# Retention and two feed-forward layers on one core: layer one's weights shared by two blocks in groups of 4, 6 and 6 steps in place of 6, 5 and 5

## The chip, the core and the metric

The kernel runs on one core of one Trainium2 chip. The metric is the device time of one execution in microseconds (us). The engines of the core are TensorE (PE, its weight loads shown as PEld), VectorE (DVE), ScalarE (ACT), GpSimd (POOL) and SyncE (SP), whose queue issues nearly all of the DMAs here. Times are medians of several runs; the profile shows one execution by itself.

## The reference, cut to what matters

```
def _attn_ref(q, k, v):                      # (4, 8, 576, 64), float32
    scores = np.matmul(q, k.transpose(0, 1, 3, 2)) / np.sqrt(64)
    gamma = 1.0 - 2.0 ** (-5.0 - np.arange(H))
    rel = pos[:, None] - pos[None, :]
    Dmat = np.where(rel >= 0, gamma[:, None, None] ** rel, 0.0)
    return np.matmul(scores * Dmat, v)

x = attn_out.transpose(0, 2, 1, 3).reshape(2304, 512)
h = x @ w_in1;  g = np.where(h > 0, h, np.exp(np.minimum(h, 0)) - 1);  y = g @ w_out1
h2 = np.maximum(y @ w_in2, 0);  out = (h2 * h2) @ w_out2
```

Both layers have 512 inputs and 2048 hidden units. The weights w_in1, w_out1, w_in2 and w_out2 come as float64 and have to be turned into float32 on the chip.

## The kernel before, in words

The 2304 tokens are cut into five blocks of 512, 512, 256, 512 and 512 tokens (BLOCKS). Every product of layer one is made of three float32r matmuls (mm3, L163 to L165): high part by high part, high by low, low by high. The 2048 hidden units of layer one are 16 pieces of 128, numbered f = 0 to 15.

**A weight unit** is one piece of w_in1 or of w_out1: 128 rows of 512 float64 values, 512 KB. Its way is: a DMA on SP's queue into a raw place (load_raw, L187 or L192); conversion to float32 (to_f32: on ACT L204 and L205, on DVE L206, L207, L208 and a custom instruction at L211); the split into high and low part (split_w: on ACT L159, on DVE L160), after which it stays in SBUF as part of a tile of three units, w0 to w10. There are 32 units, in the order in0, in1, out0, in2, out1, in3, out2, and so on to out15.

**A step** of layer one is a block and a piece f. up(blk, f) makes 12 matmuls into a PSUM tile h (two buffers), then on ACT L365 to L367 and on DVE L369 and L370 the activation, then the split of the result g (L159, L160). down(blk, f) makes 12 matmuls of g with the piece of w_out1 into four PSUM banks; it comes LAG = 2 steps later.

**Groups.** The first two blocks share each weight while it is fresh: the list GROUPS cuts the 16 pieces, and for each group block 0 runs through its pieces and then block 1 through the same pieces (ORDER1). At the end of a group down moves the four banks to SBUF (ACT copies at L404, or DVE adds at L402 where an earlier group's sums are to be added) and to the DRAM tensor parts and back (L394, L406).

**The attention** of a block runs in chunks of up to 128 tokens, each of three pieces: transposes (PE L293, ACT copies L298), scores (PE L306, DVE mask L309) and values (PE L321, L325 and L335; ACT L159 and DVE L160 write the block's x; DVE L341 or L343 update the running state st). Block 0 is done first (the list of twelve pieces with EARLY, which tells how many units are to be split after each of them). Block 1 has five chunks of 64, 128, 128, 128 and 64 tokens, so 15 pieces, and they are spread over the steps that SPREAD[1] names; they must be done before block 1's first step. The two chunks of block 2 follow at the end of the shared steps.

**The pace of conversion.** In the middle of step i (mid, called in up between the activation's ACT and DVE parts) the attention pieces of that step are emitted first and then w1_to(units1(i)): splits are emitted until units1(i) units are done. w1_run, which does it, also emits the loads and the conversions that lie ahead: a unit's conversion is one unit ahead of the splits; the loads are AHEAD_NURSED = 5 units ahead of the conversions while a unit still has a nursery place, and AHEAD = 2 ahead after that, in three rotating buffers raw_p. The nursery (NURSERY) is the SBUF of weight tiles that are not written yet: the raw units 0 to 10 land in the places of w4, w5, w6 and w10. The places of w9, w8 and w7 first hold the second, third and fourth chunk of block 0's attention.

**Order.** Loads of layer one's units and of the chunks' q, k and v stay in the order in which the code emits them on SP's queue. The other instructions are put in order by a scheduler that works before the kernel runs; on the chip each engine takes its instructions in that fixed order.

```
def w1_run(n):
    while at["split"] < min(int(n), len(w1)):
        while at["raw"] < min(at["f32"] + (AHEAD_NURSED if at["raw"] < NURSED else AHEAD), len(w1)):
            step("raw", 99, w1, lambda u: load_raw(*u))
        step("split", at["f32"], w1, split_w)
        step("f32", at["raw"], w1, to_f32)
```

Of the kernel before, what the change touches and what calls it, by code (L numbers as in the profile page):

```python
# [21 lines left out]
NF = DFF // P  # L22
# [6 lines left out]
AHEAD = 2  # L29


NURSERY = (("w4", 3), ("w5", 3), ("w6", 3), ("w10", 2))
NURSED = sum(n for _, n in NURSERY)
AHEAD_NURSED = 5

GROUPS = ((0, 6), (6, 11), (11, 16))
ORDER1 = [(b, f) for lo, hi in GROUPS for b in range(2) for f in range(lo, hi)]
SHARED = len(ORDER1)
ORDER1 += [(b, f) for b in range(2, NB) for f in range(NF)]

SPREAD = {1: (0, 5), 2: (SHARED - 5, SHARED - 1), 3: (SHARED, SHARED + NF - 2), 4: (SHARED + NF, SHARED + 2 * NF - 2)}

EARLY = (0, 0, 0, 1, 1, 2, 3, 4, 5, 6, 6, 7)


def units1(i):
    return 7 + 1.4 * min(i + 1, 5) + 0.85 * max(i - 4, 0)


def units2(i):  # L50
# [76 lines left out]
def tile_kernel(ctx: ExitStack, tc, q, k, v, w_in1, w_out1, w_in2, w_out2, cst, out):  # L127
# [43 lines left out]
    def raw_place():  # L171
# [5 lines left out]
        if len(nursery) == n:  # L177
            tag, k = NURSERY[sum(n >= sum(m for _, m in NURSERY[:i + 1]) for i in range(len(NURSERY)))]
            t = wp.tile([P, k, DM, 2], I32, tag=tag, name="raw")
# [194 lines left out]
    def down(blk, f):  # L374
        n = BLOCKS[blk][1]
        g, w = g_t.pop((blk, f)), w_t[0, 1, f]
        shared = blk < 2
        first, last = (any(f == r[e] - (e == 1) for r in (GROUPS if shared else ((0, NF),))) for e in range(2))
        if first:
            acc_t[blk] = [ps_acc.tile([P, TB], F32, tag="acc", name=f"acc{m}") for m in range(KC)]  # L380

        back = shared and last and f >= GROUPS[0][1]
        end = last and f == NF - 1
# [332 lines left out]
    def load_next(late=False):  # L716
        if at["load"] < len(chunks) and (late or chunks[at["load"]][1] < 2 or chunks[at["load"] - 1][1] >= 2):
            load_chunk(chunks[at["load"]][0])
            at["load"] += 1

    def scale_next():
        if at["scale"] < at["load"]:
            scale_chunk(chunks[at["scale"]][0])
            at["scale"] += 1
# [49 lines left out]
    pieces = ((0, 0), (1, 0), (0, 1), (1, 1), (0, 2), (2, 0), (1, 2), (3, 0), (2, 1), (3, 1), (2, 2), (3, 2))  # L774
    for (c, piece), n in zip(pieces, EARLY):
        first[c][piece]()
# [20 lines left out]
    for i, (blk, f) in enumerate(ORDER1):  # L797
        def mid():
            if i == SPREAD[2][0] - 4:
                load_next(True)  # L800
                load_next(True)
                scale_next()
            for of, (lo, hi) in SPREAD.items():
                if lo <= i < hi:
                    need = 3 * len(blocks[of])
                    for _ in range((i - lo + 1) * need // (hi - lo) - (i - lo) * need // (hi - lo)):
                        attn_step()
            if at["split"] < len(w1):
                w1_to(units1(i))
            elif i >= SHARED and at["f322"] < min(len(w2), units2(i)):  # L810

                step("park", at["f322"], w2, park_w)
                with tc.issue_after(mark[0]):
                    step("f322", at["raw2"], w2, to_f32)
                while at["raw2"] < min(len(w2), at["f322"] + 2):
                    step("raw2", 99, w2, lambda u: load_raw(*u))
            if at["f322"] == len(w2):
                step("park", 99, w2, park_w)
            j = i - (len(ORDER1) - NF)

            with tc.issue_after(mark[0]):
                if j == 6:
                    run(factors(0))
                if 7 <= j < NF and j not in (10, 14):
                    next_inputs()
# [81 lines left out]
```

## Time and profile before

| | |
|---|---|
| median of 3 runs | 896.09 us (892.68 to 896.62) |
| the profiled execution's own time | 890.18 us |
| its span, first to last instruction | 888.0 us |
| mean granted TensorE clock | 0.994 |
| busy: PE, DVE, ACT | 857.4, 686.1, 489.7 us |

The profiled execution is an execution of its own: 2.2 us of its time lie outside its span, and it is 5.9 us below the median of the other runs. Busy times of PE are modelled, because matmuls are pipelined: a row's duration is longer than the distance to the next start, and it is the distance that counts. A timeline row reads: start, duration, engine, line, operation, output and inputs, and in brackets how long the engine had been idle and on what it waited last. DVE rows too overlap by a little (0.69 us each, 0.60 us from start to start).

### The profile page before, as it was taken

How to read it: one execution, taken by the hardware profiler on the slowest of the kernel's cores; microseconds unless marked ns; L12 is line 12 of the kernel's file. 1: busy time of each engine (PE TensorE's matmuls, PEld its weight loads, DVE VectorE, ACT ScalarE, POOL GpSimd, SP SyncE). 2: the span in 40 equal slices, each digit the busy share in tenths (PEclk: the TensorE clock that was granted, in tenths of full speed). 3: DMA queues.
4: the chain of work that ended last, by engine and by line, in shares of the span. 5: the costliest groups of instructions: out<-in, count | busy, mean ns of one | idle time of the engine just before them, and what ended most of it. 6: DMA issues, size and time to landing. Idle time of an engine off the chain costs nothing.

```text
span 888.0 us, 14959 instructions
## 1 busy us (share of the span) xinstructions
PE 857.4 (97%) x5630; PEld 770.8 (87%) x5630; DVE 686.1 (77%) x1391; ACT 489.7 (55%) x961; POOL 9.2 (1%) x12
## 2 busy tenths in 40 slices
PE   8798999999998999999999999999999999999998
PEld 5676788888888988888888898999989989999997
DVE  4898888885667867766779857789874769898984
ACT  3665778673464666655767744556553434444441
POOL 3000000000000000000000000000000000000000
PEclk9999999999999999999999999999999999999999
DMA  9923426383529656534463034499997993444330
GB/s 217 272 54 108 143 96 189 119 213 96 142 61 239 160 156 186 172 109 141 132 226 94 24 111 158 154 328 345 350 323 260 401 345 131 155 147 150 120 131 37
DMA packets 157608, 155.33 MB, mean 175 GB/s; under 512 B 62816, under 2 KB 121312, under 8 KB 157536
## 3 DMA queue, kind: packets, MB, share of 16 engines
q1 hardware_dynamic: 150208, 139.69, 51.8%
q10 hardware_dynamic: 7328, 14.68, 4.6%
q8 instruction: 44, 0.72, 0.4%
q14 instruction: 28, 0.23, 0.1%
HBM read 98.77 MB, written 55.57 MB: 174 GB/s over the span
## 4 chain that ended last, share of the span: by engine, by line
PE 82%; DVE 7%; DMA 5%; ACT 2%; issue 1%; SPq 1%; ACTq 1%; POOL 0%; DVEq 0%
PE m L675 18%; PE A L492 10%; PE acc L163 7%; PE acc L164 7%; PE acc L165 7%; PE h L163 7%; PE h L165 6%; PE h L164 6%; PE D L492 5%; PE B L492 2%; PE ps_o L325 2%; PE ps_o L321 1%; DMA raw<-in_moe_w_in_dram 1%; PE ps_s L306 1%; DMA g<-g2s 1%
## 5 line engine op out<-in xcount | busy, mean ns | idle before, releaser
L675 PE MATMUL m<-wo,S 128*128 128x256 f32 x1512 | 184.2, 285 | 3.4 <-ACT S L159 2.4
L675 PEld LDWEIGHTS m<-wo,S 128*128 128x128 f32 x1512 | 183.3, 193 | 4.2 <-ACT S L159 2.8
L159 ACT CAST S<-g 128x512 fp32r<-128x512 f32 (+1 forms) x144 | 74.6, 565 | 95.7 <-DVE g L659 46.8
L163 PE MATMUL h<-x,w 128*128 128x512 f32 (+1 forms) x320 | 119.8, 376 | 3.6 <-DVE t L370 2.7
L164 PE MATMUL acc<-g,w 128*128 128x512 f32 (+1 forms) x320 | 118.8, 372 | 0.0
L164 PE MATMUL h<-x,w 128*128 128x512 f32 (+1 forms) x320 | 118.5, 370 | 0.2 <-DVE x L160 0.2
L165 PE MATMUL h<-x,w 128*128 128x512 f32 (+1 forms) x320 | 118.6, 371 | 0.0
L165 PE MATMUL acc<-g,w 128*128 128x512 f32 (+1 forms) x320 | 117.5, 370 | 0.0
L492 PE MATMUL A<-T,pair 128*128 128x384 f32 x576 | 112.9, 335 | 2.2 <-DVE go L519 1.3
L163 PE MATMUL acc<-g,w 128*128 128x512 f32 (+1 forms) x320 | 111.5, 376 | 2.8 <-ACT w L159 1.6
L492 PEld LDWEIGHTS A<-T,pair 128*128 128x128 f32 x576 | 100.6, 188 | 4.1 <-DVE go L519 2.1
L160 DVE TENSOR_TENSOR S<-g,S 128x512 fp32r<-128x512 f32 (+1 forms) x144 | 85.9, 621 | 22.3 <-ACT S L159 20.9
L365 ACT ACTIVATE t<-h 128x512 f32<-128x512 f32 (+1 forms) x80 | 44.3, 554 | 79.4 <-PE h L165 72.4
L369 DVE SCALAR_TENSOR_TENSOR t<-e,t 128x512 f32<-128x512 f32 (+1 forms) x80 | 50.8, 635 | 44.9 <-ACT t L367 44.4
L163 PEld LDWEIGHTS h<-x,w 128*128 128x128 f32 x320 | 60.5, 190 | 15.4 <-DVE t L370 3.0
L159 ACT CAST g<-t 128x512 fp32r<-128x512 f32 (+1 forms) x80 | 46.1, 578 | 46.4 <-DVE t L370 45.8
L163 PEld LDWEIGHTS acc<-g,w 128*128 128x128 f32 x320 | 59.4, 188 | 13.8 <-ACT w L159 1.8
L164 PEld LDWEIGHTS h<-x,w 128*128 128x128 f32 x320 | 60.7, 190 | 10.6 <-DVE x L160 0.4
L165 PEld LDWEIGHTS h<-x,w 128*128 128x128 f32 x320 | 60.6, 189 | 10.5 <-DVE w L160 0.2
L164 PEld LDWEIGHTS acc<-g,w 128*128 128x128 f32 x320 | 60.3, 188 | 10.3
L165 PEld LDWEIGHTS acc<-g,w 128*128 128x128 f32 x320 | 60.2, 188 | 10.0
L492 PE MATMUL D<-T,pair 128*128 128x384 f32 x288 | 58.5, 336 | 1.9 <-ACT pair L159 0.6
(88 smaller groups left out, 1280.6 us busy)
## 6 DMA issues: line engine op xcount, KB each, us to landing
g2s<-go SPq DMA_DIRECT2D x48, 384.0 KB, 4.3
g<-g2s SPq DMA_DIRECT2D x36, 512.0 KB, 3.9
raw<-in_moe_w_in_dram SPq DMA_DIRECT2D x32, 512.0 KB, 5.4
raw<-in_moe_w_out_dram SPq DMA_DIRECT2D x32, 512.0 KB, 4.1
wo2s<-wo SPq DMA_DIRECT2D x56, 256.0 KB, 4.0
wo<-wo2s ACTq DMA_DIRECT2D x9, 1536.0 KB, 15.6
w2s<-f SPq DMA_DIRECT2D x32, 256.0 KB, 2.3
f<-w2s SPq DMA_DIRECT2D x32, 256.0 KB, 4.2
```

The source lines that it names most:

```text
L159: nc.scalar.copy(pair_hi, src)
L160: eng.tensor_tensor(out=pair_lo, in0=src, in1=pair_hi.bitcast(F32), op=ALU.subtract)
L163: nc.tensor.matmul(ps, l_hi, r_hi, start=first, stop=False)
L164: nc.tensor.matmul(ps, l_hi, r_lo, start=False, stop=False)
L165: nc.tensor.matmul(ps, l_lo, r_hi, start=False, stop=last)
L306: nc.tensor.matmul(ps[e][:n, p, :n], kT[r, p, :n], qT[r, p, :n], start=True, stop=True)
L321: i = nc.tensor.matmul(ps[:, p, :n], st[:, p, :], qT[:, p, :n], start=p == 0, stop=True, skip_group_check=True)
L325: nc.tensor.matmul(ps[e * D:(e + 1) * D, p, :n], vn[:n, 2 * p + e, :], live[e][:n, p, :n], start=not s, stop=True, skip_group_check=True,)
L365: nc.scalar.activation(t, h, AF.Relu, scale=-1.0)
L369: nc.vector.scalar_tensor_tensor(out=t, in0=e, scalar=1.0, in1=t, op0=ALU.add, op1=ALU.mult)
L492: ins = nc.tensor.matmul(ps, w[:, l, o:o + P], t[:, r, j], start=first and i + j == 0, stop=i + j == 3, skip_group_check=True)
L675: ins = nc.tensor.matmul(m(u, k), l[:, x], w[:, y], start=first and k in (1, 6, 4, 5), stop=j == HF - 1 and i == 2, skip_group_check=True,)
```

## The change

The groups become 4, 6 and 6 pieces long. Block 1's attention is therefore spread over the four steps 0 to 3 and not over 0 to 4, and block 1's first step is step 4 and not step 6. EARLY asks for 6 units before step 0 and not 7. units1 asks for 0.9 unit in each of the steps 0 to 3 and 1.1 unit in each later one; before, it was 1.4 in each of the steps 0 to 4 and 0.85 later. In whole units: split before step 0, 6 (before: 7); after step 3's mid, 9 (12); after step 4's, 10 (14); after step 10's, 17 (19); all 32 after step 24's (26's). The nursery grows from 11 to 20 places by w9, w8 and w7, so that the units 11 to 19 are also loaded up to five ahead and no longer pass through raw_p.

```
-NURSERY = (("w4", 3), ("w5", 3), ("w6", 3), ("w10", 2))
+NURSERY = (("w4", 3), ("w5", 3), ("w6", 3), ("w10", 2), ("w9", 3), ("w8", 3), ("w7", 3))
 NURSED = sum(n for _, n in NURSERY)
 AHEAD_NURSED = 5
 
-GROUPS = ((0, 6), (6, 11), (11, 16))
+GROUPS = ((0, 4), (4, 10), (10, 16))
...
-SPREAD = {1: (0, 5), 2: (SHARED - 5, SHARED - 1), 3: (SHARED, SHARED + NF - 2), 4: (SHARED + NF, SHARED + 2 * NF - 2)}
+SPREAD = {1: (0, 4), 2: (SHARED - 5, SHARED - 1), 3: (SHARED, SHARED + NF - 2), 4: (SHARED + NF, SHARED + 2 * NF - 2)}
...
-EARLY = (0, 0, 0, 1, 1, 2, 3, 4, 5, 6, 6, 7)
+EARLY = (0, 0, 0, 1, 1, 2, 3, 4, 4, 5, 5, 6)
...
-    return 7 + 1.4 * min(i + 1, 5) + 0.85 * max(i - 4, 0)
+    return 6 + 0.9 * min(i + 1, 4) + 1.1 * max(i - 3, 0)
```

## Rows read from the trace of the kernel before

**Rows 1.** Busy time in four stretches: length, PE, PEld, DVE, ACT, POOL, clock, DMA.

```profile
30.00:40.00 10.00, 6.84 (x76) 5.73 (x77) 9.88 (x20) 5.35 (x10) 0.00 (x0) 1.00 1.06 284
46.00:60.00 14.00, 13.86 (x97) 11.19 (x98) 14.00 (x27) 9.20 (x18) 0.00 (x0) 1.00 0.17 36
74.00:93.00 19.00, 14.81 (x153) 11.88 (x153) 15.49 (x30) 9.86 (x20) 0.00 (x0) 1.00 0.41 128
100.00:190.00 90.00, 90.00 (x400) 74.51 (x399) 76.36 (x135) 69.78 (x124) 0.00 (x0) 1.00 0.54 154
```

**Rows 2.** PE by line, 36 to 93 us: busy, mean, idle before and its releasers.

```profile
L163 PE MATMUL h<-x,w 128*128 128x512 f32 x25 | 10.3, 419 | 1.9 <-DVE t L370 1.1 <-ACT w L159 0.7
...
L163 PE MATMUL acc<-g,w 128*128 128x512 f32 x20 | 6.3, 411 | 1.6 <-ACT w L159 1.6
L306 PE MATMUL ps_s<-qT,kT 64*128 64x128 f32 (+1 forms) x80 | 4.8, 260 | 0.7 <-ACT kT L298 0.7
L325 PE MATMUL ps_o<-P,v 128*64 128x128 f32 (+1 forms) x80 | 4.6, 257 | 0.0
L321 PE MATMUL ps_o<-qT,st 128*128 128x64 f32 (+1 forms) x32 | 4.2, 274 | 1.3 <-DVE P L309 1.3
L293 PE MATMUL ps_t<-cs,k 128*128 128x128 f32 (+1 forms) x20 | 2.7, 255 | 0.3 <-DVE st L341 0.3
L335 PE MATMUL ps_u<-v,k 128*64 128x64 f32 (+1 forms) x64 | 2.5, 221 | 0.0
L293 PE MATMUL ps_t<-cs,q 128*128 128x128 f32 (+1 forms) x16 | 2.3, 266 | 0.0
```

**Rows 3.** PE in order of time, 36 to 97 us.

```profile
36.12 0.73 PE L163 MATMUL h<-x,w 128*128 128x512 f32 x2
...
37.70 0.50 PE L164 MATMUL h<-x,w 128*128 128x512 f32 x1 [0.23 <-DVE x L160]
...
42.82 1.00 PE L321 MATMUL ps_o<-qT,st 128*128 128x64 f32 x8
...
53.52 0.39 PE L163 MATMUL h<-x,w 128*128 128x512 f32 x1
...
56.26 1.07 PE L163 MATMUL acc<-g,w 128*128 128x512 f32 x4
...
83.23 1.05 PE L321 MATMUL ps_o<-qT,st 128*128 128x128 f32 x8
...
90.65 1.10 PE L321 MATMUL ps_o<-qT,st 128*128 128x64 f32 x8 [1.28 <-DVE P L309]
...
92.84 1.22 PE L163 MATMUL h<-x,w 128*128 128x512 f32 x2
...
96.36 0.40 PE L164 MATMUL h<-x,w 128*128 128x512 f32 x1
```

**Rows 4.** SP's queue in order of time, 34 to 76 us.

```profile
34.55 0.50 SPq L192 DMA_DIRECT2D raw<-in_moe_w_out_dram  x1
...
73.67 0.60 SPq L256 DMA_DIRECT2D k<-in_k_dram  x1
74.36 0.60 SPq L256 DMA_DIRECT2D v<-in_v_dram  x1
75.01 0.61 SPq L187 DMA_DIRECT2D raw<-in_moe_w_in_dram  x1
```

**Rows 5.** ACT, then DVE, in order of time, 79 to 82 us.

```profile
79.03 0.67 ACT L204 ACTIVATE raw<-raw 128x512 int32<-128x512 uint32 x1 [2.29 <-DMA raw<-in_moe_w_in_dram]
...
80.27 0.43 DVE L206 TENSOR_SCALAR f<-f 128x512 f32<-128x512 f32 x1 [1.28 <-ACT f L205]
...
81.19 1.29 DVE L309 TENSOR_TENSOR P<-ps_s,cs 128x512 f32<-128x512 f32 x2
```

**Rows 6.** DVE in order of time, one unit's conversion and one step.

```profile
111.38 0.42 DVE L206 TENSOR_SCALAR f<-f 128x512 f32<-128x512 f32 x1
111.71 0.68 DVE L160 TENSOR_TENSOR w<-f,w 128x512 fp32r<-128x512 f32 x1
...
115.66 0.42 DVE L206 TENSOR_SCALAR f<-f 128x512 f32<-128x512 f32 x1
```

## The prediction

> **What bounds the kernel now.** I read the busy times by stretch first. From 100 to 190 us PE is busy without a gap, with DVE and ACT below it [rows 1]; there a step costs what its matmuls cost, and nothing that the change does to DVE or DMA can shorten it unless it lengthens it. The stretch that can give something back is 30 to 100 us. There DVE is the full engine at first (9.88 of 10 us, then 14.00 of 14), while from 74 to 93 us neither PE (14.81 of 19) nor DVE (15.49) is full: that part runs on waits [rows 1].
>
> The second view is PE's groups by line with what ended their idle time. From 36 to 93 us PE waits 1.1 us for L370 (the activation of an earlier step that must free a PSUM tile h), 0.7 and 1.6 us for a weight's split (ACT w), and 0.7, 1.3 and 0.3 us inside the attention, for ACT kT, DVE P and DVE st [rows 2]. The reader should see that these are small and many: 5.7 us in all.
>
> The third view is PE in order of time. Twelve matmuls of a step's half take 2.74 us (53.52 to 56.26) [rows 3]; I call that a half. Block 1's first matmul starts at 92.84, and by then PE has done 11 halves: six up, five down. The check on this book: 11 x 2.74 = 30.1 us, the attention's groups 4.8 + 4.6 + 4.2 + 2.7 + 2.5 + 2.3 = 21.1, the waits 5.7, together 56.9, against 92.84 - 36.12 = 56.7 [rows 2, 3]. So the account closes, and a gain has to come from the waits, from an earlier start, or from the clock.
>
> The fourth view, SP's queue and ACT, explains the worst of the waits. The load of unit 10 is issued at 34.55; that of unit 11 only at 75.01, behind k and v of the last chunk, which wait for buffers [rows 4]. Unit 11 is in6, which no step needs before step 12. But its conversion stands in ACT's and DVE's fixed order: ACT waits 2.29 us for the DMA at 79.03, DVE's L206 behind it 1.28 us, and only after these does the mask L309 of a chunk run at 81.19 [rows 5]; the split that PE waits for is behind them too. Work that is early holds up work that is due.
>
> **The change, part by part.** One unit and one step's activation together take DVE from 111.38 to 115.66, 4.28 us: 2.47 for the unit (five instructions) and 1.81 for the step (three) [rows 6].
>
> *EARLY asks for one unit less.* The first up stands until x of block 0 is complete (37.70, the wait for DVE x), and DVE has no gap then [rows 1, 3]. One unit less is 2.47 us of DVE work. If all of it stood ahead of x, the start comes 2.5 us earlier; if the scheduler had put it into holes, nothing. I take 1.5, nearer to the full value because DVE has only 0.12 us of holes in that stretch: -1.5 (0 to -2.5).
>
> *Group one needs four pieces, and the pace is lower.* When block 1's attention is complete the code asks for 8 splits where it asked for 12 (the last values piece stands ahead of that step's splits): four units, 9.9 us of DVE, and two steps' activation, 3.6 us, are no longer ahead of it. The 0.7 us wait is for in5's split, which group one no longer holds; the 1.6 us wait sits behind unit 11, whose conversion moves from step 2 to step 5. Both go: -2.3. The units needed in group one are split with one or two steps in hand (step 5 needs 9, and 9 are asked for in step 3). The wait for L370 is DVE running behind; with 13.5 us less in its queue I take -0.8 of 1.1 (0 to -1.1).
>
> *Five chunks in four steps.* Per step PE gets 5.48 us of halves and 21.1/4 = 5.3 of attention, DVE 0.9 x 2.47 + 1.81 and a quarter more attention per step than before. PE becomes the fuller engine, so there should be more often a half left to fill the hops of the attention. At the tail, the last chunk, PE now waits 0.7 + 1.3 + 0.3 = 2.3 us. If halves are left then, that goes; if not, it stays. I take half: -1.1 (0 to -2.3).
>
> *The clock after the tail.* The eight matmuls from 92.84 to 96.36 take 3.52 us, where eight at the usual distance (2.74/12) take 1.83: PE had idled at the tail and ran at the lower level of 1.2 GHz for a while, 1.7 us lost [rows 3]. It goes with the tail: half, -0.8 (0 to -1.7). The Trainium skill (TensorE: Matmul & The Clock Gate, Part 1) says that the throttled state is the default and activity lifts it; it prices a 512-column matmul at 427 ns there, by which eight would lose 1.6 us. That rule speaks against this change if the denser attention leaves PE idler, and the trace bears it out with the rows just read.
>
> *Nine more raw places.* Units 11 to 19 go to tiles that held chunks of block 0, read out before step 0, so nothing new waits for them. The loads can run five ahead. On SP's queue unit 11's load still stands behind chunk loads, but behind the fourth chunk's and not the fifth's, and its conversion is due later by three steps. By itself worth nothing beyond the wait already counted; if the load were late again it would cost the 2.3 us back.
>
> *The faster pace from step 4.* DVE has 1.1 x 2.47 + 1.81 = 4.5 us in a step of 5.48. That fits. But the margin of units over need shrinks from six at step 8 to none: step 15's down needs out9, the 21st, which step 14 asks for. The next half can be filled by other work, so I take +0.6; a whole unit late costs one unit's pace, 5.48/1.1 = 5.0 (0 to +5.0).
>
> *Group ends.* As many copies and adds as before, one to four steps earlier; they lie under PE's unbroken stretch [rows 1]. Zero; their price without that cover is not known from a row that isolates it.
>
> **Sum.** -1.5 - 2.3 - 0.8 - 1.1 - 0.8 + 0.6 = -5.9 us. After 100 us PE is the bound, so it is carried to the end. The profiled execution took 890.18 us (2.2 of it outside the span), so 884.3; the median of the runs is 1.0066 times the profiled time, which makes 890.1. A measurement of this kernel tells about 0.5%, 4.5 us, from no change.
>
> **Rivals.** *The attention keeps its pace, and the change is slower.* From the first chunk's values to the last's it takes 90.65 - 42.82 = 47.8 us, of which the first three hops take 13.5 each and the last 7.4 [rows 3]. Four steps hold two ups less to fill that. If those hops are the chain's own latency, block 1 starts at 92.84 - 1.5 = 91.3, with 8 halves done and not 11: lost time 91.3 - 21.9 = 69.4 against 92.84 - 30.1 = 62.7, so 6.7 us slower, 902.8. It decides from a start of block 1 at 84.6: later is a loss. For it: in the last third DVE had gaps and the hop still took 12. Against it: the last hop shows 7.4 where nothing stood in between (a 64-token chunk), the long ones had a full DVE queue or unit 11's wait in them. Chance 0.15.
>
> *The tail only moves.* The last chunk again finds no half to fill it and the clock falls again: -1.5 - 2.3 - 0.8 + 0.6 = -4.0, 892.1. For it: the last chunk is last in either order. Chance 0.20, no measurable change.
>
> *Supply fails at step 15.* One unit late, +5.0 in place of +0.6: -1.5, so 894.6. Against it: margin comes back in block 1's pass, which needs no new unit. Chance 0.08.
>
> *The prefetch does not do what it says*, because SP's order keeps the loads behind the chunks': the 2.3 us stay and the tail with them, so -5.9 + 2.3 + 1.1 + 0.8 = -1.7, 894.4. Chance 0.07.
>
> **How the numbers follow.** My forecast has 0.50, all of it counted as faster; its own range is 886 to 892 (all five gains at their bounds would be -9.9). Slower is the first rival, 0.15; the other three, 0.35, are within 0.5%. The range 885 to 898 holds the forecast, the three small rivals and a run or two of spread; it leaves out the slower rival and a little at the lower end.
>
> **What would show it.** In the profile after, block 1's first up should start near 79 us (62.7 - 1.5 - 2.3 - 0.8 - 1.1 + 21.9); the waits of PE for ACT w between 35 and 80 us should be gone; unit 11's load should be issued well before its conversion; the matmul distance behind the tail should be 0.23 us and not 0.43; PE should be without a gap up to 190 us, step 15 above all. A start of block 1 after 84.6, PE waits for w near step 15, or a longer idle stretch at the last chunk would make the forecast wrong.

## The result, and the profile after

The changed kernel takes 900.59 us (median of six runs, 898.07 to 902.55), the kernel before beside it 894.77 (six runs, 891.11 to 896.62). The ratio is 1.0073, with an interval from 1.0051 to 1.0096: slower by some 6.5 us, where the forecast was 5.9 us faster. The profiled execution took 899.88 us (span 897.7), so it lies 0.7 under its median, while that of before lies 4.6 under the median of its six. The two traces are therefore 9.7 us apart where the medians are 5.8 apart; the book below is one of traces, and the verdicts are from the runs.

Busy time by stretch in the kernel after comes first (length, PE, PEld, DVE, ACT, POOL, clock, share of DMA, GB/s), to be laid beside [rows 1]:

```profile
30.00:40.00 10.00, 9.19 (x80) 7.87 (x81) 9.85 (x21) 4.02 (x8) 0.00 (x0) 0.83 0.99 263
46.00:60.00 14.00, 12.63 (x94) 10.11 (x92) 11.57 (x20) 6.31 (x12) 0.00 (x0) 1.00 0.10 21
74.00:93.00 19.00, 14.96 (x125) 12.77 (x122) 10.26 (x20) 4.30 (x9) 0.00 (x0) 0.65 0.29 104
100.00:190.00 90.00, 89.50 (x396) 73.79 (x395) 81.01 (x149) 72.07 (x130) 0.00 (x0) 1.00 0.46 148
```

From 74 to 93 us PE is as busy as before (14.96 us against 14.81), but the clock granted there averages 0.65 where it was 1.00, and PE does 125 matmuls in place of 153. Busy time alone hides this: the same matmul counts for longer. DVE fell from 15.49 to 10.26 us, as the forecast wanted, and nothing came of it. From 100 to 190 us PE is full but for half a microsecond, so what is lost by 100 us stays lost.

The clock is not a feature of this one trace. The median granted clock is 0.984 over the six runs of the changed kernel and 0.989 to 0.990 over the runs of the kernel before in the five sittings of the experiments. The share that is missing to full speed, times the span, is 14.4 us in the changed kernel and 8.9 to 9.8 us before (medians). An estimate from these figures: the clock can account for up to about 5 of the 6.5 us; it is an upper bound, because a low clock costs nothing while PE waits.

PE's groups by line from 35 to 88.6 us, against [rows 2]:

```profile
L163 PE MATMUL h<-x,w 128*128 128x512 f32 x17 | 7.2, 432 | 0.1
...
L321 PE MATMUL ps_o<-qT,st 128*128 128x64 f32 (+1 forms) x32 | 6.1, 353 | 2.2 <-DVE P L309 2.2
L306 PE MATMUL ps_s<-qT,kT 64*128 64x128 f32 (+1 forms) x80 | 6.0, 303 | 1.9 <-ACT kT L298 1.9
L325 PE MATMUL ps_o<-P,v 128*64 128x128 f32 (+1 forms) x80 | 5.7, 297 | 0.0
...
L163 PE MATMUL acc<-g,w 128*128 128x512 f32 x12 | 5.0, 455 | 0.0
...
L293 PE MATMUL ps_t<-cs,q 128*128 128x128 f32 (+1 forms) x20 | 3.0, 278 | 3.4 <-DVE x L160 1.9 <-DVE st L343 1.6
L335 PE MATMUL ps_u<-v,k 128*64 128x64 f32 (+1 forms) x64 | 3.0, 244 | 0.0
L293 PE MATMUL ps_t<-cs,k 128*128 128x128 f32 (+1 forms) x20 | 2.7, 258 | 0.6 <-DVE st L341 0.6
```

The waits on a split (ACT w) and on L370 are gone. In their place every wait sits inside the attention: 2.2 + 1.9 + 1.9 + 1.6 + 0.6 = 8.2 us, against 2.3 before. The attention's own groups grew from 21.1 to 6.1 + 6.0 + 5.7 + 3.0 + 2.7 + 2.4 = 25.9 us. (The 2.4 is the row of q's transposes without the four matmuls at 34.71, which start before the first up; the rows of before leave these four out as well.) Their means grew with them: L321 from 274 to 353 ns, L306 from 260 to 303.

PE in order of time, against [rows 3]:

```profile
35.51 0.73 PE L163 MATMUL h<-x,w 128*128 128x512 f32 x2
...
41.91 1.00 PE L321 MATMUL ps_o<-qT,st 128*128 128x64 f32 x8
...
57.07 1.09 PE L325 MATMUL ps_o<-P,v 128*64 128x128 f32 x16
...
62.15 1.84 PE L306 MATMUL ps_s<-qT,kT 64*128 64x128 f32 x16 [0.67 <-ACT kT L298]
63.92 0.79 PE L163 MATMUL acc<-g,w 128*128 128x512 f32 x1
...
66.74 1.07 PE L165 MATMUL acc<-g,w 128*128 128x512 f32 x4
...
67.65 1.05 PE L321 MATMUL ps_o<-qT,st 128*128 128x128 f32 x8
68.63 1.09 PE L325 MATMUL ps_o<-P,v 128*64 128x128 f32 x16
69.55 0.64 PE L335 MATMUL ps_u<-v,k 128*64 128x64 f32 x16
71.14 0.66 PE L293 MATMUL ps_t<-cs,q 128*128 128x128 f32 x4 [0.95 <-DVE x L160]
71.99 0.63 PE L293 MATMUL ps_t<-cs,k 128*128 128x128 f32 x4 [0.20 <-DVE st L341]
73.33 1.16 PE L306 MATMUL ps_s<-qT,kT 64*128 64x128 f32 x16 [0.72 <-ACT kT L298]
76.16 2.08 PE L321 MATMUL ps_o<-qT,st 128*128 128x128 f32 x8 [1.67 <-DVE P L309]
78.17 1.73 PE L325 MATMUL ps_o<-P,v 128*64 128x128 f32 x16
79.73 0.63 PE L335 MATMUL ps_u<-v,k 128*64 128x64 f32 x16
...
83.12 1.12 PE L306 MATMUL ps_s<-qT,kT 64*64 64x64 f32 x16 [0.51 <-ACT kT L298]
84.74 1.97 PE L321 MATMUL ps_o<-qT,st 128*128 128x64 f32 x8 [0.50 <-DVE P L309]
...
88.54 1.22 PE L163 MATMUL h<-x,w 128*128 128x512 f32 x2
...
92.97 0.48 PE L163 MATMUL h<-x,w 128*128 128x512 f32 x1
```

Read it from the middle. The last half of block 0 (a down) ends at 67.65, and from there to 88.54, 21 us, PE has nothing but the attention's own matmuls, eight of the fifteen groups behind a wait for ACT or DVE. Eight matmuls of L321 take 0.98 us at 67.65 (to 68.63) and 2.01 at 76.16 (to 78.17): between these two the clock fell from 2.4 to 1.2 GHz. It had fallen once before, behind an earlier stretch with the attention alone (57.07 to 62.15): the scores take 1.84 us at 62.15 and 1.16 at 73.33, and the last half of block 0, from 63.92 to 67.65, takes 3.73 us and not 2.74. It rises for a while (0.63 us at 79.73, as at 69.55), falls again by 83.12 (1.12 us for scores that took 0.68 in the kernel before) and is low when block 1 starts: ten matmuls of layer one, from 88.54 to 92.97, take 4.43 us where ten at full pace take 10 x 2.74 / 12 = 2.28. Block 1's first matmul comes at 88.54, 4.3 us earlier than before (92.84), but with 7 halves done and not 11.

SP's queue, against [rows 4]: the load of unit 11 is now issued at 59.77, where it was 75.01.

```profile
59.77 0.94 SPq L187 DMA_DIRECT2D raw<-in_moe_w_in_dram  x1
```

**The book.** By the prediction's own account, time lost by block 1's start is 88.54 - 7 x 2.74 = 69.4 us against 62.7. This is the number of the first rival (69.4 against 62.7, 6.7 us slower), but that the two agree to the tenth is luck: the rival had a start at 91.3 with 8 halves, and the trace has 88.54 with 7. With the loss behind the tail (2.15 against 1.70) the difference is 7.1 us. At the activation (L365) of step 11 after lies 7.1 us behind, at the end of layer one 7.4. The other 2.3 of the 9.7 come later; the first matrix products of the next stage (L492, A) hold 1.5 of them in busy time and 0.6 in waits, and no experiment looked into these. The busy part is the clock again: it was 0.50 from 670 to 672 us, and 1.00 in the same stage of the trace before (656 to 668). The trace of e9, which keeps the groups of before, has such a drop there too (0.57 from 660 to 664), so it is no mark of the new groups.

### The profile page after: what moved, and what is told of

Its sections match the earlier page's. It is cut to its first block, busy times and chain, and to the rows that moved or that the text cites. A ratio compares the mean times of both kernels' runs of the same rounds, so it can differ in the third digit from the quotient of the medians.

```text
span 897.7 us, 14965 instructions
## 1 busy us (share of the span) xinstructions
PE 863.7 (96%) x5630; PEld 777.1 (87%) x5630; DVE 684.7 (76%) x1391; ACT 489.8 (55%) x961; POOL 8.6 (1%) x12
## 3 DMA queue, kind: packets, MB, share of 16 engines
q1 hardware_dynamic: 150208, 139.69, 51.2%
## 4 chain that ended last, share of the span: by engine, by line
PE 78%; DMA 8%; DVE 7%; ACT 3%; SPq 2%; issue 1%; ACTq 1%; DVEq 0%
PE m L675 18%; PE A L492 9%; PE h L163 7%; PE acc L163 6%; PE acc L164 6%; PE h L164 6%; PE h L165 6%; PE acc L165 6%; PE D L492 4%; PE B L492 2%; DMA raw<-in_moe_w_in_dram 2%; DMA wo<-wo2s 2%; PE ps_o L325 2%; PE ps_o L321 1%; PE ps_s L306 1%
## 5 line engine op out<-in xcount | busy, mean ns | idle before, releaser
L164 PE MATMUL acc<-g,w 128*128 128x512 f32 (+1 forms) x320 | 118.7, 373 | 0.1
L492 PE MATMUL A<-T,pair 128*128 128x384 f32 x576 | 114.4, 339 | 2.8 <-DVE go L519 2.0
L165 PE MATMUL acc<-g,w 128*128 128x512 f32 (+1 forms) x320 | 116.3, 368 | 0.0
L163 PE MATMUL acc<-g,w 128*128 128x512 f32 (+1 forms) x320 | 109.1, 376 | 2.1 <-DVE x L402 1.7
L492 PEld LDWEIGHTS A<-T,pair 128*128 128x128 f32 x576 | 101.9, 190 | 4.9 <-DVE go L519 2.8
L365 ACT ACTIVATE t<-h 128x512 f32<-128x512 f32 (+1 forms) x80 | 44.4, 554 | 74.2 <-PE h L165 68.0
L164 PEld LDWEIGHTS h<-x,w 128*128 128x128 f32 x320 | 60.8, 190 | 10.2 <-issue 0.2
L492 PE MATMUL D<-T,pair 128*128 128x384 f32 x288 | 58.5, 336 | 2.0 <-ACT pair L159 0.7
```

The costliest lines, as they stand in the source:

```text
L163: nc.tensor.matmul(ps, l_hi, r_hi, start=first, stop=False)
L164: nc.tensor.matmul(ps, l_hi, r_lo, start=False, stop=False)
L165: nc.tensor.matmul(ps, l_lo, r_hi, start=False, stop=last)
L365: nc.scalar.activation(t, h, AF.Relu, scale=-1.0)
L492: ins = nc.tensor.matmul(ps, w[:, l, o:o + P], t[:, r, j], start=first and i + j == 0, stop=i + j == 3, skip_group_check=True)
```

## The experiments

Two theories stood at the start. A: the groups carry the loss. Block 0's halves are used up while block 1's attention runs on, so the same loss comes with the groups alone and goes if PE gets other work in those gaps. B: the new pace or the new places carry it, by late units or by loads that displace others. All ratios are against the kernel before, run on the same chip in the same rounds.

### The three parts alone

**e1_groups_only**, the kernel before with the groups of the change:

```
-GROUPS = ((0, 6), (6, 11), (11, 16))
+GROUPS = ((0, 4), (4, 10), (10, 16))
-SPREAD = {1: (0, 5), ...
+SPREAD = {1: (0, 4), ...
```

> The kernel before with the groups of 4, 6 and 6 steps and block 1's attention over four steps, nothing else. Theory A (the attention's chain of five chunks has too little other matmul work beside it: 7 halves of a step and not 11): slower than before by 5 to 8 us, block 1's first up starts with 7 halves done and the matmul clock at its lower level around it. Theory B (the slower pace of conversion leaves the chain without weights): no slower than before, within 2 us.

899.04 against 893.93, ratio 1.0050 [1.0034, 1.0067]. The groups alone make it slower by 4.5 us by the ratio and 5.1 between the medians, at the low end of A's 5 to 8. Block 1 starts at 90.33 with 8 halves, not 7: the eighth goes with the pace (e6 has it too). A holds.

**e2_pace_only**, the kernel before with the change's pace:

```
-EARLY = (0, 0, 0, 1, 1, 2, 3, 4, 5, 6, 6, 7)
+EARLY = (0, 0, 0, 1, 1, 2, 3, 4, 4, 5, 5, 6)
...
-    return 7 + 1.4 * min(i + 1, 5) + 0.85 * max(i - 4, 0)
+    return 6 + 0.9 * min(i + 1, 4) + 1.1 * max(i - 3, 0)
```

> The kernel before with the changed EARLY and the changed pace of conversion alone, groups of 6, 5 and 5. Theory A: not slower by itself, 0 to 3 us faster, since DVE gets four units less ahead of block 1's first step and eleven halves stay. Theory B: slower by 4 us or more, with PE waiting for ACT w in the first group.

895.74, ratio 1.0027 [1.0009, 1.0045]: 2.4 us slower by the ratio, which is neither A (no loss) nor B (4 us or more). A group of 6 needs its fifth and sixth piece earlier than this pace makes them. The waits of PE from 30 to 100 us (total, times, longest) show it; before had 1.6 and 0.7 in the same two places [rows 2]:

```profile
PE acc L163 <- ACT w L159: 4.8, 3, 2.9
...
PE h L163 <- ACT w L159: 1.3, 2, 0.7
```

The longest of them, 2.86 us at 97.42, lies behind the attention's end.

**e3_places_only** and **e9_places_again**, the kernel before with the nine places alone, run in two sittings:

```
-NURSERY = (("w4", 3), ("w5", 3), ("w6", 3), ("w10", 2))
+NURSERY = (("w4", 3), ("w5", 3), ("w6", 3), ("w10", 2), ("w9", 3), ("w8", 3), ("w7", 3))
```

> The kernel before with the nine more raw places alone. By the prediction's reading of the wait for unit 11: its load is emitted two steps earlier, ACT's wait of 2.3 us for it and PE's 1.6 us wait behind it go, 1 to 3 us faster. If the load stays behind the chunk loads on SP's queue: no change, within 1 us.

> The kernel before with the nine places alone once more, for an execution near its median in the profile (the first profile was of its slowest execution). Theory A: 4 to 6 us faster than before again; the gain stands in the stretch from 60 to 100 us, where ACT no longer waits for unit 11's load and block 1's first step comes 3 to 5 us earlier; after that the two kernels keep their distance.

888.95 against 893.93, ratio 0.9949 [0.9931, 0.9967], and 889.7 against 893.52, ratio 0.9948 [0.9927, 0.9968]. This part alone is 4 to 5 us faster than the kernel before, more than the 1 to 3 expected of e3, and by the ratios 11 faster than the whole change. In e9 the load of unit 11 is issued at 60.46, and ACT's wait for a raw load (2.29 us in [rows 5]) is not among its waits any more. PE's wait for ACT w at the downs, 1.6 us in [rows 2], is half as long from 30 to 100 us:

```profile
ACT x L159 <- PE ps_o L325: 9.6, 4, 4.6
ACT w L159 <- DVE f L211: 7.6, 4, 2.6
...
PE acc L163 <- ACT w L159: 0.8, 1, 0.8
```

Block 1 starts at 91.68 with 11 halves, 1.2 us earlier than before. The profile of before is a quick execution of its kernel (890.18) and e9's a usual one (889.79), so the traces do not show where the whole of the 4 to 5 us comes from.

**e5_no_places**, the change without the nine places (NURSERY as before):

> The changed kernel without the nine more raw places (groups and pace alone). The parts measured alone sum to 5.1 + 1.8 - 5.0 = +1.9 us, the whole change is near +6.5. Theory A says that the places pay only in the groups of 6, 5 and 5, where unit 11's load held up work of the first group; in the first group of four that unit is not due any more. Then this kernel takes the same time as the changed one, within 1.5 us. If the parts simply add, it is 5 us slower than the changed kernel, near 905.

899.1 against 892.35, ratio 1.0067 [1.0038, 1.0097], as the whole change. The places that are worth 0.5% with groups of 6, 5, 5 are worth nothing here that the intervals can tell. It fits that with this pace the work they speed up is no longer ahead of block 1; no run isolates that. The parts do not add up: +0.50, +0.27 and -0.51% make 0.26%, and the whole is 0.73%.

**e6_groups_places**, the change with the pace of before:

> The changed kernel with EARLY and the pace of before. Theory A: its first group gets out3 split in time and so an eighth half beside the attention (seven in the changed kernel), worth 2 to 4 us: near 897, still slower than before. If the parts add: 0 us against before.

902.68, ratio 1.0102 [1.0077, 1.0127]. The expectation failed. An eighth half does run, but ACT, in order of time, meets a new wait:

```profile
84.72 0.59 ACT L404 COPY part<-acc 128x512 f32<-128x512 f32 x1 [3.71 <-DMA parts<-part]
85.20 0.59 ACT L159 CAST x<-ps_o 128x512 fp32r<-128x512 f32 x1
```

A copy of the group's end waits 3.71 us for a store, and block 1's x stands right behind it in ACT's order. The start slips to 94.03. The clock is part of it: 0.54 from 74 to 94 us.

### Work for the gaps

**e4_after_fill**, the changed kernel, with matmuls added in block 1's last three chunks behind the transposes, scores and values. They write a PSUM tile that nobody reads:

```
+        def fill(l, r):
+            if blk == 1 and b == 1 and s:
+                no = ps_h.tile([P, TB], F32, tag="h", name="no")
...
+                nc.tensor.matmul(o_, l, r, start=True, stop=True)
...
+            fill(qk[:, :P], qk[:, :2 * P])
...
+            fill(kT[:, 0, :n], kT[:, :, :n])
...
+            fill(live[1][:n, 0, :n], live[1][:n, :, :n])
```

> The changed kernel with matmuls added that nobody reads, in block 1's chunks from the third on: one of 256 columns at the transposes, one of up to 512 at the scores and at the values, in float32, into a free h buffer. Theory A with the clock as its price: some 5 of the 7 us lost come from matmuls at the lower level of the clock, so with PE kept busy the granted clock stays at 2.4 GHz and the kernel is 2 to 5 us faster than the changed kernel although PE does more. If it is the waits themselves and not the clock: no faster than the changed kernel, or slower by up to 3 us.

893.47 against 893.93, ratio 0.9993 [0.9977, 1.0010]: more work, and by the ratios about 7 us less time than the changed kernel. Its stretch from 74 to 93 us (columns as above):

```profile
74.00:93.00 19.00, 18.19 (x154) 14.19 (x153) 12.82 (x24) 8.94 (x17) 0.00 (x0) 1.00 0.28 100
```

The clock stays at full speed, block 1 starts at 86.72 with the same 7 halves (1.8 us earlier), and the ten matmuls behind the tail take 2.41 us and not 4.43. Theory A holds here too: with other work in the gaps the loss goes. The median granted clock of its twelve runs is 0.994, above the kernel before, and PE's waits inside the attention are 3.7 us where the changed kernel has 8.2. One caveat: the scheduler also moved an up of block 0 to between the scores and the values of the fourth chunk (73.96 to 77.13), where it fills a hop. How much of the gain is the clock's and how much that half's is open.

**e7_places_fill**, the same added matmuls in the places-alone kernel:

> The kernel before with the nine places and with the matmuls that nobody reads in block 1's chunks. Theory A with the clock as the price: the places' 5 us and the 2 us of lower clock behind the last chunk add: 886 to 888 us. If PE is the bound in group one with eleven halves, the added matmuls (some 10 us of them) stand in the way: slower than with the places alone, 890 or more.

897.43 against 892.35, ratio 1.0055 [1.0035, 1.0075]: some 9 us slower than the places alone by the ratios (1.07%). Where PE has halves to run, added matmuls only stand in their way.

### Other group sizes

**e12_groups_565** (groups of 5, 6, 5, all else as before) and **e8_groups_754** (7, 5, 4 with the nine places and the pace of before):

```
e12: +GROUPS = ((0, 5), (5, 11), (11, 16))
e8:  +GROUPS = ((0, 7), (7, 12), (12, 16))
     +SPREAD = {1: (0, 6), ...
```

> The kernel before with groups of 5, 6 and 5, all else as before, so block 1's attention stays on five steps and keeps nine halves beside it (eleven before, eight with the groups of 4, 6 and 6 alone). Theory A: between the two, 1 to 4 us slower than before. If the number of halves beside the chain does not matter: the same as before, or faster.

> Groups of 7, 5 and 4, block 1's attention over six steps, the nine places, the pace of before. Theory A, taken the other way: thirteen halves can stand beside the same attention, so the waits and the low clock of the first group shrink further: 885 to 888 us, faster than the places alone (889). Against it: block 1's attention no longer bounds the group, and DVE's conversions do: the same as the places alone, or slower.

e12: 897.49 against 893.52, ratio 1.0046 [1.0029, 1.0064]. e8: 894.55 against 892.35, ratio 1.0007 [0.9986, 1.0028], which is some 5 us worse than the places with groups of 6, 5, 5. A first group of 5 costs, and one of 7 does not help, so the number of halves does not order the kernels by itself. In e12 all downs of block 0's first group are done before block 1 starts, and the copies at the group's end stand on ACT ahead of the last chunk's qT and kT. PE's longest wait of that stretch is behind them (ACT, then PE):

```profile
86.12 1.54 ACT L404 COPY part<-acc 128x512 f32<-128x512 f32 x3
```

```profile
88.75 1.12 PE L306 MATMUL ps_s<-qT,kT 64*64 64x64 f32 x16 [2.10 <-ACT kT L298]
```

In e8's trace PE waits once for L370 behind block 1's start (1.6 us at 112.20), where e9 has no such wait; that is a part of its loss at most, and the rest is open.

### The length of the chain

If the attention's chain sets block 1's start only after the change, a longer chain should cost only there.

**e10_after_hop** and **e11_before_hop**, the changed kernel and the kernel before, each with a second, in-place copy of qT and kT on ACT in block 1's chunks:

```
                 nc.scalar.copy(tt[:, :, :n], ps[:, :, :n])
+                if blk == 1:
+                    nc.scalar.copy(tt[:, :, :n], tt[:, :, :n])
```

> The changed kernel with each of block 1's copies out of PSUM after the transposes followed by a second copy in place on ACT: some 5 us more on the way from a chunk's transposes to its scores, over the five chunks. Theory A (block 1's start is set by the length of the attention's chain): slower than the changed kernel by 4 us or more, and more than the same edit costs in the kernel before. If block 1's start is set by the sum of PE's work: slower by under 2 us.

> The same second copies in the kernel before. Theory A: its eleven halves hide most of the hops but those of the last chunk: slower than before by 0 to 2.5 us, clearly less than in the changed kernel. If the chain sets block 1's start here too: 4 us or more.

902.32 against 893.52, ratio 1.0101 [1.0078, 1.0124], and 897.96, ratio 1.0054 [1.0034, 1.0074]. The longer hop costs 0.54% over the kernel before and 0.28% over the changed kernel (1.0101 against 1.0073, each known to about 0.0023). The second is not clear of noise and the difference between the two is not either, but the expected larger cost in the changed kernel did not show. So "only after the change" falls: in the kernel before block 1's start moves as well, from 92.84 to 100.30 with the same 11 halves. That the chain sets it there is argued and not shown, because the edit also gives ACT more work.

Two ways were tried to shorten the chain, each in the changed kernel, the kernel before and the places-alone kernel. **e13_after_dve**, **e14_before_dve** and **e15_places_dve** give the copy of kT in block 1 to DVE; **e16_after_pool**, **e17_before_pool** and **e18_places_pool** give the scaling of block 1's q and k to GpSimd:

```
e13 to e15:
+                if blk == 1 and nm == "kT":
+                    nc.vector.tensor_copy(tt[:, :, :n], ps[:, :, :n])
+                else:
+                    nc.scalar.copy(tt[:, :, :n], ps[:, :, :n])
e16 to e18:
-        eng = nc.gpsimd if ch in blocks[0] else nc.vector
+        eng = nc.gpsimd if ch in blocks[0] + blocks[1] else nc.vector
```

> The changed kernel with the copy of kT of block 1's chunks moved from ACT to DVE, so that it runs beside the copy of qT: up to 0.6 us less in each of three hops and 0.4 in two. If the chain sets block 1's start: 1.5 to 3 us faster than the changed kernel, 897 to 898.5. If the start is set by something else: the same within 1 us.

> The same move in the kernel before. If the chain sets block 1's start in both kernels and DVE is no limit: 1.5 to 3 us faster than before, as in the changed kernel. If DVE's backlog is what makes the chain long here (DVE was full to 70 us): no gain, or slower by up to 3 us, since DVE gets five instructions more.

> The kernel before with the nine places and the same move. The version that could beat both kernels: the places' 4.5 us and the hop's gain, if there is one in e14, add to 886 to 888 us; if DVE is the limit, 889 to 892.

> The changed kernel with the scaling of q and k of block 1's chunks on GpSimd and not on DVE. If DVE's fixed order is part of the chain (its waits of 1.28 and 1.35 us for k): 1 to 3 us faster than the changed kernel. If the chain is its own hops alone: the same within 1 us, or slower where GpSimd's longer instruction (1.04 us for 0.6) is late.

> The same in the kernel before. If DVE's backlog makes the chain long here: DVE loses ten instructions of 0.6 us before block 1's start, 2 to 5 us faster than before. If not: the same within 1 us.

> The kernel before with the nine places and the scaling on GpSimd: if e17 gains, the two add, 885 to 888 us; otherwise 889 to 891.

| edit | changed kernel | kernel before | places alone |
|---|---|---|---|
| none | 1.0073 [1.0051, 1.0096] | 1 | 0.9948 [0.9927, 0.9968] |
| kT on DVE | 1.0146 [1.0118, 1.0173] | 1.0079 [1.0054, 1.0105] | 1.0075 [1.0046, 1.0104] |
| scaling on GpSimd | 1.0108 [1.0078, 1.0137] | 1.0069 [1.0046, 1.0092] | 1.0030 [1.0009, 1.0052] |

None gains. Five of the six are slower than the same kernel without the edit; e16's 0.35% over the changed kernel is within the noise. The stretch from the first up to block 1's start grew in e13 (60.8 us against 53.0), e14 and e17 (65.1 and 64.7 against 56.7) and e15 (65.8 against 55.9 and 58.6 in the two traces of the places alone); in e18 and e16 it did not (58.7; 51.9 against 53.0). e13 shows how a move can lengthen the chain, on DVE in order of time and then on PE:

```profile
81.56 0.68 DVE L267 TENSOR_TENSOR k<-k,cs 64x512 f32<-64x512 f32 x1 [1.13 <-DMA k<-in_k_dram]
82.28 0.69 DVE L299 COPY kT<-ps_t 128x512 f32<-128x512 f32 x1
```

```profile
83.11 2.08 PE L309 MATMUL ps_s<-qT,kT 64*128 64x128 f32 x16 [1.91 <-DVE kT L299]
```

The copy landed behind the scaling of the next chunk's k, which waits 1.13 us for its load, and PE's scores wait 1.91 us for the copy (0.72 for ACT's at 73.33 above). On GpSimd the scaling can be slow. Three scalings of 128 rows in e17, in order of time:

```profile
44.48 3.86 POOL L267 TENSOR_TENSOR q<-q,cs 128x512 f32<-128x512 f32 x1 [7.41 <-DMA q<-in_q_dram]
48.30 4.65 POOL L267 TENSOR_TENSOR k<-k,cs 128x512 f32<-128x512 f32 x1
...
66.70 1.04 POOL L267 TENSOR_TENSOR k<-k,cs 128x512 f32<-128x512 f32 x1 [12.30 <-DMA k<-in_k_dram]
```

The same instruction takes 0.68 us on DVE. Whether a chain that is really shorter would make any of the three faster was not settled.

### One account for all of them

The same book, kept from each trace: block 1's start, less 2.74 us for each half done by then, plus what the ten matmuls behind the tail take beyond 2.28 us. Against it stands the profiled execution of the same trace, both as differences from the kernel before (64.4 by the book, 890.18 profiled).

| kernel | first up | halves | start of block 1 | book, us | profiled, us |
|---|---|---|---|---|---|
| places alone (e9) | 35.80 | 11 | 91.68 | -0.7 | -0.4 |
| places alone (e3) | 37.78 | 11 | 96.39 | +3.5 | +3.1 |
| groups 7, 5, 4 (e8) | 36.58 | 13 | 99.54 | +1.7 | +4.5 |
| groups 5, 6, 5 (e12) | 35.17 | 10 | 94.17 | +4.5 | +4.6 |
| groups alone (e1) | 37.07 | 8 | 90.33 | +6.2 | +7.9 |
| the change | 35.51 | 7 | 88.54 | +7.1 | +9.7 |
| the change without places (e5) | 37.09 | 7 | 93.10 | +10.9 | +13.0 |
| the change, pace of before (e6) | 35.92 | 8 | 94.03 | +9.9 | +12.3 |
| the change with fill (e4) | 36.06 | 7 | 86.72 | +3.3 | +2.0 |
| the change with a hop (e10) | 38.62 | 7 | 95.84 | +14.4 | +16.6 |
| before with a hop (e11) | 36.55 | 11 | 100.30 | +7.9 | +8.4 |
| the change, scaling on GpSimd (e16) | 36.61 | 7 | 88.53 | +6.3 | +11.0 |

The book follows the profiled times within about 3 us in all of these but e16, which is 4.7 us off. The same holds for e13, e14, e15, e17 and e18; e7 is left out, because its attention ends in the middle of a half. The pace alone (e2) is the other place where it does not: -0.3 by the book and +5.6 profiled, so that part of the loss lies behind the tail, where its wait of 2.86 us stands. The two executions of the places alone are 4.2 us apart in the book and 3.5 in time, so a difference of a few us between two traces says little of the kernels.

Read the stretch from the first up to block 1's start: 53.0 us with 7 halves, 53.3 with 8 (e1), 59.0 with 10, 56.7 with 11, 63.0 with 13. Four halves less should have made it 11.0 us shorter, and it is 3.7 us shorter. It is no fixed length: with 7 halves it is 56.0 us in e5, and 50.7 in e4, where the clock stays up. PE's own work in it is, with the attention at 21.1 us, 40.3 us with 7 halves (7 x 2.74 + 21.1) and 51.2 with 11. With 11 the work nearly fills the stretch; with 7 it does not, and PE waits, slows down, and does the missing halves afterwards.

## Why the prediction was wrong, by its own steps

**EARLY asks for one unit less: -1.5.** The first up came 0.6 us earlier (36.12 to 35.51). Kernels with the same code up to there show as much difference between executions (37.78 in e3, 35.80 in e9), so no gain can be read here.

**Group one needs four pieces, the pace is lower: -2.3 and -0.8.** Right. PE's waits for ACT w in this stretch are gone (2.3 us before, none longer than 0.1 now), and L370's 1.1 us too (e6, with the pace of before, still has 1.1). The load of unit 11 moved ahead as foreseen (59.77).

**Five chunks in four steps: -1.1.** This is the step that failed. "PE becomes the fuller engine, so there should be more often a half left to fill the hops" weighed the work per step: 5.48 us of halves against 5.3 of attention. It did not ask how many halves there are at all before block 1 may start, nor where the order puts them. The prediction's sums had 8 halves there. There are 7, they are used up by 67.65, and the last 21 us of the attention run without any. Waits inside the attention went from 2.3 to 8.2 us: +5.9 in place of -1.1. The groups alone carry most of the loss (e1), and work in those gaps takes it back (e4).

**The clock after the tail: -0.8.** Wrong in sign, and looked for in the wrong place. Behind the tail the loss went from 1.70 to 2.15 us, +0.45. The larger price is in the attention, where the same matmuls took 25.9 us and not 21.1, +4.8. The prediction's sum had no term for it. The rule of the Trainium skill that the prediction weighed (TensorE: Matmul & The Clock Gate, Part 1: the throttled state is the default, activity lifts it; 427 ns for 512 columns) agrees with the trace: the matmuls behind 88.54 stand 0.43 us apart.

**Nine more raw places: 0.** Not contradicted inside this change (e5). It hid that the places are worth 0.5% by themselves: they are the only part that gains, and beside the other two nothing of it is left to see.

**The faster pace from step 4: +0.6.** The size came out, but not for the reason given. PE waits for no weight near step 15. Its one wait from 100 to 190 us is 0.50 us for L370 at 175.80, before step 20's up. Ahead of it ACT had waited 1.61 and 3.24 us for raw loads:

```profile
163.80 0.68 ACT L204 ACTIVATE raw<-raw 128x512 int32<-128x512 uint32 x1 [1.61 <-DMA raw<-in_moe_w_out_dram]
...
168.27 0.66 ACT L204 ACTIVATE raw<-raw 128x512 int32<-128x512 uint32 x1 [3.24 <-DMA raw<-in_moe_w_in_dram]
```

SP had issued these loads at 159.12 and 163.21, behind the stores (155.84 to 158.67) and reads (162.79) of a group's end. **Group ends: 0.** They have a hand in this half microsecond. Where they fall into the attention they cost more: 3.71 us of ACT's time in e6 and 2.10 of PE's in e12.

In the traces the terms make -0.6 - 2.3 - 1.0 + 5.9 + 4.8 + 0.45 + 0.5 = +7.8 us, of 9.7 (roughly, because PE's rows overlap). But they are not how the start was bought: these waits and slow matmuls are what remains of the stretch when there are four halves fewer. Four halves are 11.0 us that now come after the start, and the start came 4.3 earlier: 6.7 us slower. That is the outcome of the first rival, which was given a chance of 0.15, though not its mechanism in full: the attention did not keep its pace. The argument against it ("the last hop shows 7.4 where nothing stood in between") was true and not enough: after the change the two last hops take 8.5 and 8.6 us (67.65 to 76.16, 76.16 to 84.74), no longer the 13.5 of before, and from the first values to the last it is 42.8 us in place of 47.8; but with 7 halves done the start would have had to come at 62.7 + 7 x 2.74 = 81.9 (the prediction's 84.6 was for 8). The rival also had no term for the clock inside the attention. That a longer chain moves the start is not new with the change, as e11 suggests. What is new is that the halves no longer suffice to run beside it.

Still open: the share of the clock and that of the moved half in e4, why a first group of 7 loses too, whether a shorter chain would help, and where all of the places' gain lies.

## What to carry to other kernels

Where a fixed amount of work may run beside a chain of dependent steps, count what is there in all and where the order puts it, not its rate per step: a piece taken away from beside the chain has to be done afterwards, and the chain gets shorter by less than that piece. Here 11 halves and the attention, 51.2 us of PE, nearly fill a stretch of 56.7; with 7 halves, PE's 40.3 us stand in a stretch of 53.0. Test a change of several parts by its parts: the kernel before with the nine places alone, 0.9948 [0.9927, 0.9968], beats both kernels.

## What the hardware showed that was not expected

PE's busy share of a stretch does not tell its clock, because a matmul at the lower level counts for longer. From 74 to 93 us PE was busy 14.96 of 19 us at 0.65 of full speed after the change, and 14.81 of 19 us at 1.00 before it. No single wait in the slow stretch was longer than 1.67 us. What PE had done before the clock fell (from 67.65 to 76.16, busy 4.98 of 8.51 us) was the attention's matmuls alone, of at most 128 columns, with waits of 0.2 to 1.67 us between the groups. With unread matmuls of 256 and 512 columns among them, and one half of layer one, the granted clock of that stretch was 1.00 (e4).

The scaling of q or k of 128 rows, 0.68 us on DVE, took 1.04 us on GpSimd at 66.70 in e17, and 3.86 and 4.65 us from 44.48 to 52.91; e18 has the same (4.52 and 4.65 us from 46.05). DVE was full beside all three (3.00 of 3 us from 46 to 49, 4.00 of 4 from 49 to 53, 2.97 of 3 from 65 to 68), so that alone does not decide it. DVE can pay as well: its L208 at 82.02 in e17, beside k's scaling on GpSimd from 81.97 to 83.01, took 1.54 us and not 0.69. So an edit that should relieve DVE came out as a loss; which of the two engines pays, and when, no run isolates.
